# Cosine attention and MLP mixer on one core: two channel groups begun a slot earlier, token mixing in bunches, a cast moved, the last group halved

## The chip, the core and the metric

The kernel runs on one NeuronCore of a Trainium2 chip. The metric is the time on the device of one execution, in microseconds (us). Before the change the median of three runs is 408.05 us.

The engines have names in two styles. TensorE (PE in the profile) multiplies matrices. VectorE is DVE, ScalarE is ACT, GpSimd is POOL, and SyncE is SP, which issues most of the transfers. Each engine works through its own instructions in order; semaphores tie the engines together. TensorE writes only to PSUM, and all other tiles lie in SBUF.

## The reference, cut to what matters

```python
q_n = q / (norm(q) + 1e-6);  k_n = k / (norm(k) + 1e-6)      # 8 batches, 12 heads, 448 x 64
attn = softmax(q_n @ k_n.T / tau)                            # tau = 0.1
x = (attn @ v), heads side by side                           # 8 x 448 x 768
h = relu(x.T @ w_tok1) @ w_tok2                              # 448 -> 256 -> 448, along the sequence
u = x + h.T
out = u + relu(u @ w_ch1) @ w_ch2                            # 768 -> 1536 -> 768, along the channels
```

Inputs and output are float32. The kernel holds the operands of all matrix products as float16 and sums in float32.

## The kernel before

**Attention in slots.** Two heads make a pair; a batch has 6 pairs (`NPAIR`), and 8 batches have 48 (`N`). The main loop runs over slots, one pair a slot: in slot i the scores and exponentials of pair i are made, the product with v of pair i-1 (`pv`, in two parts), and the norms and transposes of the pairs to come. Nothing is scheduled by a planner: the order of the calls in the source is the order on each engine.

Slots 0 to 12 run `opening(i)`. On TensorE a slot there is: `score(i, 0)` (4 matmuls of 448 columns, L261, tile pS), `pv(i-1)` (32 matmuls of 65 columns, L282, tile pO), `score(i, 1)`, and `tpose_pe(i+1)` (8 transposes of the next pair, L240, tile pT). VectorE copies pT to the tile qkT (L248), which `score(i+1, 0)` reads. ScalarE makes the exponentials, `expo(i, 0)` to `expo(i, 3)` (L268, 112x896 each). POOL squares q and k (L180) and scales them (`normalize`, L213) with the reciprocal that VectorE makes (`norm_rec`, L200 and L202). VectorE also sums the squares (`norm_sum`, L190, tile ssq), casts v (`recast`, L127, a tensor_reduce over an axis of length 1), and scales pO into x (L288 and L289). From slot 13 on, `slot(i)` does the same with the transposes by DMA (`tpose_dma`, on SP's queue).

**Mixing.** `mixer(b)` makes the jobs of batch b:

- token mixing, first product: `tok1` (4 matmuls of 384 columns, L313, tile pR; ReLU on ScalarE to tile r, L316), four jobs;
- token mixing, second product: `tok2(i, dh)` (L326 or, for tile 3, L331; tile pU), then the sum with x on VectorE (L335, tile u, float32); after the second half of a tile the cast to float16, on VectorE for odd i (L339) and on ScalarE for even i (L341), and a transpose of the cast tile by DMA to the tile uT, on SP's queue;
- channel mixing, first product: `ch1(ct)` (a group of 6 matmuls, L379, tile pG; ReLU on ScalarE to gT, L381), twelve jobs;
- channel mixing, second product: `ch2(i, dh)` (a group of 12 matmuls of 384 columns, L388, tile pF; sum on VectorE, L392; then the store).

An even batch has three tiles of 128 rows, an odd one four; tile 3 holds the last 64 rows of both. So an odd batch has eight `tok2` jobs and an even one six.

For batch 0 the token mixing is not in the queue: it is done a pair at a time within slots 2 to 6 (`tok1_pair`, L351; `tok2_pair`, L362; `u_pair`, L370). `u_pair` writes the float16 sum of one pair and starts its transpose to `uT[:, pj]` on SP's queue. The sixth of the `uT` parts, `DT` = 6, is that of the last pair.

**The queue of jobs.** `spread(jobs, 6)` puts jobs into the list `todo` and sets `gap`, the sum of their costs over 30. `fill()`, called five times a slot, adds `gap` to a credit and pops jobs while the credit is above zero. After slot 6 the list is an empty job of 1.6 and the first eight `ch1` jobs of batch 0; the other four are kept as `late`. After slots 12, 18, 24, ... the list is what is late, the token jobs of the next batch merged with `ch2` jobs of the batch before (`held`), and the `ch1` jobs of the next batch. For an odd batch the merge gives four `tok1`, one `ch2`, four `tok2`, one `ch2`, four `tok2`, four `ch2`. What is left at the end runs after the last slot.

**PSUM.** The pool `ps` has four buffers, shared by pT, pO, pR, pU, pG and pF; `pss` has two for the scores. A tile waits until a buffer has been read out.

**Weights.** w_tok1 and w_tok2 are loaded in float32 and cast: `w1_cast` on VectorE, `w2_cast(0)` and `w2_cast(1)` on ScalarE (L139), in slots 1 and 2, each ahead of `score(i, 1)` and the exponentials that follow it. w_ch1 and w_ch2 come by DMAs from POOL's queue in slots 1 to 11.

Of the kernel before, what the change touches and what calls it, by code (L numbers as in the profile page):

```python
# [9 lines left out]
FP32 = mybir.dt.float32  # L10
FP16 = mybir.dt.float16
AF = mybir.ActivationFunctionType
ALU = mybir.AluOpType
# [10 lines left out]
def kernel(  # L24
# [19 lines left out]
    nc = tc.nc  # L44

    B, H, S, E = q.shape
    D = H * E
# [249 lines left out]
    def mixer(b):  # L297
        e, g = b % 2, b // 2
        xt = x16[g]
        t0, nt = (0, 3) if e == 0 else (3, 4)  # L300
        W = nt * 128
        r16[b] = mix.tile([128, TT, D], FP16, name="r16", tag="r16", bufs=2)
        u32 = mix.tile([128, nt, D], FP32, name="u32", tag="u32", bufs=2)
        u16 = mix.tile([128, nt, D], FP16, name="u16", tag="u16")
        uT = mix.tile([128, DT, W], FP16, name="uT", tag="uT")
        gT = mix.tile([128, CT, W], FP16, name="gT", tag="gT")

        def tok1(tt, dh):
            def job():
                pR = ps.tile([128, DH], FP32, name="pR", tag="ps")  # L310
                ks = [(4 * e + t, t) for t in range(3)] + [(3, 3 + e)]
                for n, (xi, wi) in enumerate(ks):
                    nc.tensor.matmul(pR[:], w1t[:, wi, tt * 128:(tt + 1) * 128],  # L313
                                     xt[:, xi, dh * DH:(dh + 1) * DH],
                                     start=(n == 0), stop=(n == 3))
                nc.scalar.activation(out=r16[b][:, tt, dh * DH:(dh + 1) * DH], in_=pR[:],  # L316
                                     func=AF.Relu)
            return 0.66, job

        def tok2(i, dh):  # L320
            def job():
                pU = ps.tile([128, DH], FP32, name="pU", tag="ps")
                for tt in range(TT):
                    if i != 3:
                        c0 = 128 * (i % 4)
                        nc.tensor.matmul(pU[:], w2t[:, tt, c0:c0 + 128],  # L326
                                         r16[b][:, tt, dh * DH:(dh + 1) * DH],
                                         start=(tt == 0), stop=(tt == TT - 1))
                    else:
                        for h in range(2):  # L330
                            nc.tensor.matmul(pU[64 * h:64 * h + 64], w2t[:, tt, S - 64:S],  # L331
                                             r16[2 * g + h][:, tt, dh * DH:(dh + 1) * DH],
                                             start=(tt == 0), stop=(tt == TT - 1))
                cols = slice(dh * DH, (dh + 1) * DH)
                nc.vector.tensor_tensor(out=u32[:, i - t0, cols], in0=pU[:], in1=xt[:, i, cols],  # L335
                                        op=ALU.add)
                if dh == NDH - 1:
                    if i % 2:
                        nc.vector.tensor_copy(out=u16[:, i - t0, :], in_=u32[:, i - t0, :])  # L339
                    else:  # L340
                        nc.scalar.copy(out=u16[:, i - t0, :], in_=u32[:, i - t0, :])  # L341
                    nc.sync.dma_start_transpose(
                        out=uT[:, :, (i - t0) * 128:(i - t0 + 1) * 128], in_=u16[:, i - t0, :])
            return 0.33, job

        def tok1_pair(pj):
            cols = slice(2 * pj * E, 2 * pj * E + 128)
            pR = ps.tile([128, TT, 128], FP32, name="pR", tag="ps")
            for tt in range(TT):
                for t in range(4):  # L350
                    nc.tensor.matmul(pR[:, tt, :], w1t[:, t, tt * 128:(tt + 1) * 128],  # L351
                                     xt[:, t, cols], start=(t == 0), stop=(t == 3))
            nc.scalar.activation(out=r16[b][:, :, cols], in_=pR[:], func=AF.Relu)

        pUs = {}

        def tok2_pair(pj):
            cols = slice(2 * pj * E, 2 * pj * E + 128)
            pU = ps.tile([128, nt, 128], FP32, name="pU", tag="ps")
            for i in range(nt):  # L360
                for tt in range(TT):
                    nc.tensor.matmul(pU[:, i, :], w2t[:, tt, i * 128:(i + 1) * 128],  # L362
                                     r16[b][:, tt, cols], start=(tt == 0), stop=(tt == TT - 1))
            pUs[pj] = pU

        def u_pair(pj, half):
            cols = slice(2 * pj * E, 2 * pj * E + 128)
            u = u16[:].rearrange("p t d -> p (t d)").rearrange("p (j x) -> p j x", j=NPAIR)[:, pj]
            o = u.rearrange("p (t e) -> p t e", t=nt) if half else u32[:, :, cols]
            nc.vector.tensor_tensor(out=o, in0=pUs[pj][:], in1=xt[:, 0:nt, cols], op=ALU.add)  # L370
            if half:
                nc.sync.dma_start_transpose(
                    out=uT[:, pj, :].rearrange("d (t m) -> d t m", t=nt), in_=u)

        def ch1(ct):
            def job():
                pG = ps.tile([128, W], FP32, name="pG", tag="ps")
                for dt in range(DT):
                    nc.tensor.matmul(pG[:], wc1t[:, dt, ct * 128:(ct + 1) * 128], uT[:, dt, :],  # L379
                                     start=(dt == 0), stop=(dt == DT - 1))  # L380
                nc.scalar.activation(out=gT[:, ct, :], in_=pG[:], func=AF.Relu)  # L381
            return 6 * W / 2400, job

        def ch2(i, dh):
            def job():
                pF = ps.tile([128, DH], FP32, name="pF", tag="ps")
                for ct in range(CT):
                    nc.tensor.matmul(pF[:], gT[:, ct, (i - t0) * 128:(i - t0 + 1) * 128],  # L388
                                     wc2t[:, ct, dh * DH:(dh + 1) * DH],
                                     start=(ct == 0), stop=(ct == CT - 1))  # L390
                o = u32[:, i - t0, dh * DH:(dh + 1) * DH]
                nc.vector.tensor_tensor(out=o, in0=pF[:], in1=o, op=ALU.add)  # L392
                end = b == B - 1 and i == t0 + nt - 1
                if dh == NDH - 1 or end:
                    store(i, slice(dh * DH, (dh + 1) * DH) if end else slice(0, D), end)
            return 1.96, job

        def store(i, cols, end):
            if i == 3:
                parts = [(h, 64 * h, S - 64, 64) for h in range(2)]  # L400
            else:
                f0 = 128 * (i % 4)
                parts = [(e, f - f0, f, n) for f, n in f_segments(f0, f0 + 128)]
            for z, (h, m, f, n) in enumerate(parts):
                rows = out[2 * g + h].rearrange("(p c) d -> c p d", c=NCH)
                queue = nc.scalar if end and z else nc.sync
                queue.dma_start(out=rows[f // P, f % P:f % P + n, cols],
                                in_=u32[m:m + n, i - t0, cols])

        if b == 0:  # L410
            front = (tok1_pair, tok2_pair, u_pair)
        else:
            front = [tok1(tt, dh) for dh in range(NDH) for tt in range(TT)]
            front += [tok2(i, dh) for i in range(t0, t0 + nt) for dh in range(NDH)]
        return (front, [ch1(ct) for ct in range(CT)],
                [ch2(i, dh) for i in range(t0, t0 + nt) for dh in range(NDH)])

# [58 lines left out]
    def opening(i):  # L476
# [10 lines left out]
        squares(i + 3)  # L487
        if i in wide:
            wide[i]()
        fill()  # L490
        if i >= 1:
            pv(i - 1, 0)
            pv(i - 1, 1)
        norm_rec(i + 2)
        if i in (1, 2):
            w2_cast(i - 1)
        r_, u_, add = first[0] if first else (None,) * 3
        done = [i - 2] if 2 <= i <= NPAIR else []
        if done:
            r_(i - 2)  # L500
# [1 line left out]
        score(i, 1)  # L502
        expo(i, 2)
        expo(i, 3)
        tpose_pe(i + 1)
        if i == NPAIR:
            r_(i - 1)
# [1 line left out]
        for pj in done:  # L509
            u_(pj)  # L510
        if i == NPAIR + 1:
            first[0][2](NPAIR - 1, False)
        for half in (True, False):
            for pj in done:
                if half or pj != NPAIR - 1:
# [46 lines left out]
    for i in range(N + 1):  # L562
# [13 lines left out]
                tpose_dma(i + 1)  # L576
            slot(i)
        if i == NPAIR:
            spread([(1.6, lambda: None)] + first[1][:8], NPAIR)
            late, held = first[1][8:], first[2]  # L580
        elif i and i % NPAIR == 0:
            front, c1, c2 = mixer(i // NPAIR - 1)
            spread(late + merge(front, held[:-3]) + held[-3:] + c1, NPAIR)
            late = []
            held = c2
    for _, job in todo + held:
# [36 lines left out]
```

## Time and profile before

| | |
|---|---|
| median of 3 runs | 408.05 us (406.93 to 409.0) |
| the profiled execution, in all | 408.18 us |
| its span, first to last instruction | 406.0 us |
| TensorE busy | 382.7 us, 94% of the span |
| ScalarE busy | 261.5 us, 64% |
| VectorE busy | 234.7 us, 58% |
| POOL busy | 196.2 us, 48% |
| granted TensorE clock, mean | 0.994 |

The times in all views are microseconds from the start of the span. A line of the timeline gives start, duration, engine, source line, operation, output and inputs, shapes and count; a bracket at its end gives the idle time of the engine before it and who ended it. Several equal instructions that follow each other are merged into one line. TensorE's matmuls overlap, so that a merged duration is a little longer than the time from its start to the next line's start. The chain of waits goes back from the last instruction to what released it, and gives time on the chain instead of durations.

### The profile page before, as it was taken

The page shows a single profiled execution, that of the slowest core. Times are in us where ns is not written, and L with a number is a line of the kernel's source. Part 1 is how long each engine was busy: PE and PEld are TensorE (multiplying, and loading weights), DVE is VectorE, ACT ScalarE, POOL GpSimd, SP SyncE. Part 2 cuts the span into 40 slices and gives each one's busy share as a digit, 9 for nine tenths or more (in the row PEclk, how much of TensorE's full clock was granted, in tenths as well). Part 3 has the DMA queues.
Part 4 walks back from the last instruction along what each step waited for, and adds up shares of the span by engine and source line. Part 5 has one row for each costly group of instructions (what it writes and reads, how often), then busy time and mean ns, then how long its engine had stood idle before and what let it go on. Part 6 is the DMA issues. An engine that isn't in the chain of part 4 may idle for free.

```text
span 406.0 us, 8998 instructions
## 1 busy us (share of the span) xinstructions
PE 382.7 (94%) x3592; PEld 219.4 (54%) x3592; DVE 234.7 (58%) x534; ACT 261.5 (64%) x451; POOL 196.2 (48%) x205
## 2 busy tenths in 40 slices
PE   2798799899999999999999999999999999999996
PEld 1465566555545555555555565555545556655453
DVE  5879978557544765467634766558644773161022
ACT  6799879865767557856687567756676665521400
POOL 3979979826544647443734655644653520000000
PEclk9999989999999999999999999999999999999999
DMA  7999999939963698529773597539972352026023
GB/s 240 260 234 213 227 293 227 242 99 190 228 135 92 160 216 203 139 79 199 225 185 101 144 189 233 131 80 191 245 157 68 78 123 84 2 61 134 0 48 109
DMA packets 97305, 63.57 MB, mean 157 GB/s; under 512 B 57520, under 2 KB 93808, under 8 KB 97264
## 3 DMA queue, kind: packets, MB, share of 16 engines
q1 hardware_dynamic: 93952, 58.14, 59.7%
q0 software_dynamic: 3184, 4.72, 6.7%
q8 instruction: 28, 0.46, 0.5%
q14 instruction: 13, 0.11, 0.1%
q10 hardware_dynamic: 128, 0.15, 0.1%
HBM read 43.38 MB, written 11.01 MB: 134 GB/s over the span
## 4 chain that ended last, share of the span: by engine, by line
PE 81%; DVE 12%; DMA 4%; ACT 2%; issue 1%; SPq 0%; DVEq 0%
PE pG L379 27%; PE pF L388 27%; PE pO L282 10%; PE pS L261 9%; PE pR L313 5%; PE pU L326 3%; DVE ssq L190 2%; DVE x L289 2%; DMA kl<-in_k_dram 1%; DVE qkT L248 1%; DVE u L370 1%; ACT pE L268 1%; DMA ql<-in_q_dram 1%; DMA w2s<-in_moe_w_tok_dram 1%; DVE u L335 1%; DVE rec L288 1%
## 5 line engine op out<-in xcount | busy, mean ns | idle before, releaser
L268 ACT ACTIVATE pE<-pS 112x896 f16<-112x896 f32 x192 | 164.8, 913 | 35.3 <-PE pS L261 34.7
L379 PE MATMUL pG<-uT,wc1t 128*128 128x384 f16 (+1 forms) x576 | 121.4, 355 | 0.0
L388 PE MATMUL pF<-wc2t,gT 128*128 128x384 f16 x672 | 116.6, 326 | 0.2
L213 POOL TENSOR_TENSOR qkn<-ql,rn 112x512 f16<-112x512 f32 x47 | 49.0, 1043 | 130.6 <-DVE rn L202 109.6
L388 PEld LDWEIGHTS <-gT 128*128 128x128 f16 x672 | 63.5, 98 | 47.0 <-issue 7.3
L381 ACT ACTIVATE gT<-pG 128x384 f16<-128x384 f32 (+1 forms) x96 | 52.4, 547 | 44.8 <-PE pG L379 43.9
L379 PEld LDWEIGHTS <-wc1t 128*128 128x128 f16 x576 | 51.6, 98 | 51.4 <-issue 11.0
L392 DVE TENSOR_TENSOR u<-pF,u 128x384 f32<-128x384 f32 x56 | 31.1, 555 | 78.0 <-PE pF L388 77.7
L261 PE MATMUL pS<-qkT 64*112 64x448 f16 x384 | 60.3, 385 | 9.8 <-DVE qkT L248 5.1
L282 PEld LDWEIGHTS <-pE 112*128 112x128 f16 x1536 | 59.0, 99 | 16.1 <-issue 5.6
L282 PE MATMUL pO<-v,pE 112*128 112x65 f16 x1536 | 62.8, 196 | 0.0
L288 DVE RECIPROCAL rec<-pO 128x6 f32<-128x6 f32 x96 | 17.5, 182 | 76.1 <-PE pO L282 75.2
L190 DVE TENSOR_REDUCE ssq<-sq 112x16 f32<-112x1024 f32 (+1 forms) x50 | 58.5, 1171 | 4.2 <-ACT sq L178 3.1
L180 POOL TENSOR_TENSOR sq<-ql 112x512 f32<-112x512 f32 x46 | 48.7, 1058 | 5.6 <-DMA ql<-in_q_dram 5.6
L213 POOL TENSOR_TENSOR qkn<-kl,rn 112x512 f16<-112x512 f32 x47 | 49.0, 1042 | 0.0
L180 POOL TENSOR_TENSOR sq<-kl 112x512 f32<-112x512 f32 x46 | 48.3, 1051 | 0.0
L289 DVE TENSOR_TENSOR x<-pO,rec 128x384 f16<-128x384 f32 x96 | 40.9, 426 | 3.3
L261 PEld LDWEIGHTS <-qkT 64*112 64x112 f16 x384 | 19.1, 128 | 35.6 <-issue 22.6
L127 DVE TENSOR_REDUCE v<-vl 112x512 f16<-112x512 f32 x40 | 25.5, 640 | 0.0
L335 DVE TENSOR_TENSOR u<-pU,x 128x384 f32<-128x384 f32 x50 | 25.4, 545 | 0.1
L341 ACT CAST u<-u 128x768 f16<-128x768 f32 x14 | 11.6, 832 | 20.9 <-DVE u L335 20.9
L194 ACT ACTIVATE ln<-ssq 112x16 f32<-112x16 f32 (+1 forms) x49 | 10.9, 222 | 17.5 <-DVE ssq L190 17.2
(43 smaller groups left out, 183.4 us busy)
## 6 DMA issues: line engine op xcount, KB each, us to landing
ql<-in_q_dram SPq DMA_DIRECT2D x48, 224.0 KB, 3.6
kl<-in_k_dram SPq DMA_DIRECT2D x48, 224.0 KB, 4.0
vl<-in_v_dram SPq DMA_DIRECT2D x48, 224.0 KB, 4.2
out_dram<-u SPq DMA_DIRECT2D x8, 336.0 KB, 3.4
wc1t<-in_moe_w_ch_dram POOLq DMA_DIRECT2D x4, 576.0 KB, 7.9
wc2t<-in_moe_w_ch_dram POOLq DMA_DIRECT2D x3, 768.0 KB, 10.1
out_dram<-u SPq DMA_DIRECT2D x8, 288.0 KB, 3.8
out_dram<-u SPq DMA_DIRECT2D x7, 240.0 KB, 3.0
```

The source lines that it names most:

```text
L180: nc.gpsimd.tensor_mul(out=s["sq"][:, j], in0=a, in1=a)
L190: nc.vector.tensor_reduce(out=small(i, "ssq")[:, j], in_=st_[i]["sq"][:, j], axis=AXX.X, op=ALU.add)
L213: eng.tensor_tensor(out=t[:, j].rearrange("p c g e -> p g c e"), in0=s[nm][:], in1=_bcast_free(rn, E), op=ALU.mult)
L261: nc.tensor.matmul(pS[:, h, 0:S], s["T"][64 * h:64 * h + 64, 1, c * P:(c + 1) * P], s["T"][64 * h:64 * h + 64, 0, :], start=True, stop=True)
L268: nc.scalar.activation(out=s["p"][:, c], in_=s["pS"][c][:, :, 0:S], func=AF.Exp, scale=inv_tau)
L282: nc.tensor.matmul(pO[:, n, h, :], s["p"][:, c, h, c0:c0 + 128], s["v16"][:, NCH * h + c, 0:E + 1], start=(c == 0), stop=(c == NCH - 1))
L289: nc.vector.tensor_tensor(out=xt[hp:hp + nr, t0:t0 + len(ts), d0:d0 + 2 * E].rearrange("p t (h e) -> p t h e", h=2), in0=pO[m0:128, :, :, ...
L335: nc.vector.tensor_tensor(out=u32[:, i - t0, cols], in0=pU[:], in1=xt[:, i, cols], op=ALU.add)
L379: nc.tensor.matmul(pG[:], wc1t[:, dt, ct * 128:(ct + 1) * 128], uT[:, dt, :], start=(dt == 0), stop=(dt == DT - 1))
L381: nc.scalar.activation(out=gT[:, ct, :], in_=pG[:], func=AF.Relu)
L388: nc.tensor.matmul(pF[:], gT[:, ct, (i - t0) * 128:(i - t0 + 1) * 128], wc2t[:, ct, dh * DH:(dh + 1) * DH], start=(ct == 0), stop=(ct == C ...
L392: nc.vector.tensor_tensor(out=o, in0=pF[:], in1=o, op=ALU.add)
```

## The change

There are five edits.

1. The first two `ch1` groups of batch 0 leave the queue. In slot 7 (`NPAIR + 1`), after the transposes of pair 8, their matmuls over parts 0 to 3 of uT are issued; in slot 8, ahead of the first `fill`, those over parts 4 and 5 and the two ReLUs. The queue after slot 6 holds `ch1` jobs 2 to 9 instead of 0 to 7, and two jobs are late instead of four.
2. `w2_cast(0)` stands behind `expo(1, 2)` and `expo(1, 3)` in slot 1. `w2_cast(1)` stays.
3. For odd batches the token jobs stand in another order among the `ch2` jobs: four `tok1` and two `tok2`, one `ch2`, three `tok2`, one `ch2`, three `tok2`, four `ch2`.
4. The cast of u to float16: tiles 1 and 5 on VectorE as a tensor_reduce instead of a copy; tile 3 on ScalarE instead of VectorE; the other tiles stay on ScalarE.
5. The very last `ch2` group is computed as two groups of 12 matmuls of 192 columns, each with its own sum and its own stores.

```diff
-                    if i % 2:
-                        nc.vector.tensor_copy(out=u16[:, i - t0, :], in_=u32[:, i - t0, :])
+                    if i in (1, 5):
+                        recast(u16[:, i - t0, :], u32[:, i - t0, :])
                     else:
                         nc.scalar.copy(out=u16[:, i - t0, :], in_=u32[:, i - t0, :])
...
+        def ch1_part(ct, d0, d1):
+            if not d0:
+                pGs[ct] = ps.tile([128, W], FP32, name="pG", tag="ps")
+            for dt in range(d0, d1):
+                nc.tensor.matmul(pGs[ct][:], wc1t[:, dt, ct * 128:(ct + 1) * 128], uT[:, dt, :],
+                                 start=(dt == 0), stop=(dt == DT - 1))
+            if d1 == DT:
+                nc.scalar.activation(out=gT[:, ct, :], in_=pGs[ct][:], func=AF.Relu)
+
         def ch1(ct):
...
+            return 6 * W / 2400, partial(ch1_part, ct, 0, DT)
...
                 end = b == B - 1 and i == t0 + nt - 1
-                if dh == NDH - 1 or end:
-                    store(i, slice(dh * DH, (dh + 1) * DH) if end else slice(0, D), end)
+                parts = 2 if end and dh == NDH - 1 else 1
+                for z in range(parts):
+                    cols = slice(dh * DH + z * DH // parts, dh * DH + (z + 1) * DH // parts)
+                    pF = ps.tile([128, DH // parts], FP32, name="pF", tag="ps")
+                    for ct in range(CT):
+                        nc.tensor.matmul(pF[:], gT[:, ct, (i - t0) * 128:(i - t0 + 1) * 128],
+                                         wc2t[:, ct, cols],
+                                         start=(ct == 0), stop=(ct == CT - 1))
+                    o = u32[:, i - t0, cols]
+                    nc.vector.tensor_tensor(out=o, in0=pF[:], in1=o, op=ALU.add)
+                    if end:
+                        store(i, cols, end)
+                if dh == NDH - 1 and not end:
+                    store(i, slice(0, D), end)
...
+        if i == NPAIR + 2:
+            for ct in range(2):
+                first[0][3](ct, DT - 2, DT)
         fill()
...
-        if i in (1, 2):
-            w2_cast(i - 1)
+        if i == 2:
+            w2_cast(1)
...
         expo(i, 2)
         expo(i, 3)
+        if i == 1:
+            w2_cast(0)
         tpose_pe(i + 1)
...
         if i == NPAIR + 1:
-            first[0][2](NPAIR - 1, False)
+            add(NPAIR - 1, False)
+            for ct in range(2):
+                g_(ct, 0, DT - 2)
...
         if i == NPAIR:
-            spread([(1.6, lambda: None)] + first[1][:8], NPAIR)
-            late, held = first[1][8:], first[2]
+            spread([(1.6, lambda: None)] + first[1][2:10], NPAIR)
+            late, held = first[1][10:], first[2]
         elif i and i % NPAIR == 0:
             front, c1, c2 = mixer(i // NPAIR - 1)
-            spread(late + merge(front, held[:-3]) + held[-3:] + c1, NPAIR)
+            if (i // NPAIR) % 2:
+                mid = merge(front, held[:-3]) + held[-3:]
+            else:
+                mid = front[:6] + held[:1] + front[6:9] + held[1:2] + front[9:] + held[2:]
+            spread(late + mid + c1, NPAIR)
```

In the changed kernel's traces `ch1`'s matmuls are at L381 and its ReLU at L384, `ch2`'s matmuls at L397 and its sum at L401.

More of the change, by code (lines that the diff above doesn't have):

```diff
@@ L373, in u_pair @@
                     out=uT[:, pj, :].rearrange("d (t m) -> d t m", t=nt), in_=u)
-        def ch1(ct):
[L376 to L382, printed above, removed]
+        pGs = {}
@@ L384, in ch2 @@
         def ch2(i, dh):
             def job():
[L386 to L392, printed above, removed]
@@ L410, in mixer @@
         if b == 0:
-            front = (tok1_pair, tok2_pair, u_pair)
+            front = (tok1_pair, tok2_pair, u_pair, ch1_part)
         else:
@@ L494, in opening @@
         norm_rec(i + 2)
-        if i in (1, 2):
-            w2_cast(i - 1)
-        r_, u_, add = first[0] if first else (None,) * 3
+        if i == 2:
+            w2_cast(1)
+        r_, u_, add, g_ = first[0] if first else (None,) * 4
         done = [i - 2] if 2 <= i <= NPAIR else []
```

## The prediction

> **What bounds the kernel now.** I read the page first, parts 2 and 4.
>
> ```profile
> span 406.0 us, 8998 instructions
> ...
> PE   2798799899999999999999999999999999999996
> ...
> PEclk9999989999999999999999999999999999999999
> ...
> PE 81%; DVE 12%; DMA 4%; ACT 2%; issue 1%; SPq 0%; DVEq 0%
> ```
>
> One character is 10.15 us. From the eighth (71 us) TensorE is full to the end; before that it has gaps, and in the sixth slice its clock fell. So work taken out of the full part counts in full, and work put into an early gap is free if nobody waits behind it. The fall is at slots 7 and 8; the timeline and the windows show it.
>
> ```profile
> 47.29 0.57 PE L240 MATMUL pT<-id,qkn 112*128 112x112 f16 x8
> 48.77 0.62 DVE L248 COPY qkT<-pT 128x896 f16<-128x896 f16 x1
> 49.45 0.63 PE L261 MATMUL pS<-qkT 64*112 64x448 f16 x4 [1.59 <-DVE qkT L248]
> 50.02 2.10 PE L379 MATMUL pG<-uT,wc1t 128*128 128x384 f16 x6
> 53.48 0.20 DVE L288 RECIPROCAL rec<-pO 128x6 f32<-128x6 f32 x1 [1.90 <-PE pO L282]
> 54.57 1.14 PE L379 MATMUL pG<-uT,wc1t 128*128 128x384 f16 x6
> ...
> 46.57:49.98 3.41, 1.59 (x16) 1.00 1.26 274
> 49.98:53.40 3.42, 3.42 (x35) 0.50 1.13 220
> ...
> 32.92:36.33 3.41, 2.69 (x39) 1.00 1.39 191
> ```
>
> Slot 7 ends with 1.59 us in which TensorE waits for VectorE's copy of the transposed pair. The window lines read: stretch, its length, TensorE busy (instructions), granted clock, DMA. The stretch with 1.59 us of work is followed by one of 3.42 us at half clock; a stretch with 2.69 us was not. So six pG matmuls took 2.04 us on the chain there, against 0.98 later, and VectorE waited for pO until 53.48.
>
> The timeline and the chain around 180 us show the second place:
>
> ```profile
> 179.53 1.37 DVE L339 CAST u<-u 128x768 f16<-128x768 f32 x1
> 185.08 0.56 DVE L339 CAST u<-u 128x768 f16<-128x768 f32 x1
> 184.18 0.50 PE L326 MATMUL pU<-r,w2t 128*128 128x384 f16 x2 [0.65 <-DVE x L289]
> ```
>
> In batch 3 VectorE falls behind four token products in a row and a slow cast, and TensorE waits for a PSUM buffer. Batch 5 repeats it at 272 to 277. By matmul starts, TensorE loses 0.22, 0.25 and 0.82 us over its usual pace, 1.28 per batch.
>
> **The change part by part.** Durations are of the profiled execution: 406.0 in the span, 408.18 in all, so 2.1 outside; the median is 408.05, so I subtract gains from that.
>
> *The w2 cast, slot 1.* Now:
>
> ```profile
> 17.51 0.99 ACT L139 CAST w2t<-w2s 128x448 f16<-128x448 f32 x1 [1.01 <-DMA w2s<-in_moe_w_tok_dram]
> 18.40 3.35 ACT L268 ACTIVATE pE<-pS 112x896 f16<-112x896 f32 x4
> ```
>
> Two exponentials stand behind a wait of 1.01 for a load and the 0.99 cast. Put ahead, they start at 17.1, when their scores are done, and end at 18.8; the cast follows to 19.8. The next score waits for them and for the copy of 18.45 to 19.07: it starts at 19.1 instead of 19.37, its second half 0.65 earlier. pv, VectorE and POOL behind it follow. ScalarE itself gains only 0.3, but its next exponentials had gaps before them. Gain 0.65 (0.2 to 0.7) up to slot 7, where slots 3 to 6 keep a VectorE rhythm of 4.44.
>
> *Two groups begun in slot 7.* Eight pG matmuls go between the transposes and score(8,0). At 0.162 each (the rate inside a group) that is 1.30. They wait for two PSUM buffers, freed by VectorE at 47.70 and 48.23, and for the transposed pair 3, issued at 39.90 and landed 7.2 later, at 47.1. So they run from 47.7 to 49.1 and are over before VectorE's copy ends at 49.39. score(8,0), queued behind them, is not late. All that makes them free is this gap; without it they cost 1.30.
>
> *The same groups ended in slot 8.* Four matmuls (0.65) now precede the group that the queue pops there. They need pair 5, whose transpose was issued at 46.22 and landed 4.3 later, at 50.5. The stretch before 49.98 now holds 1.59 + 1.30 = 2.89 us of work, more than the 2.69 that stayed warm, so I take full clock. If the landing stays at 50.5: the last three run to 50.98, a group 0.98, three quarters of pv 0.74: pO at 52.70 against 53.45, a gain of 0.75 that contains the cast's 0.65. If the landing moves up by 0.65 with its issue, 1.40. I take 1.1 for both edits together. ScalarE gets three ReLUs (0.49 each) ahead of expo(8,2); they end at 53.4, expo(8,2) started at 54.09. The second pv half and the next transposes wait for the first two ReLUs, done by 52.9, before they are needed. Slots 9 to 12 pass the 1.1 on: POOL, 4.8 a slot and full, starts 55.45 on VectorE's reciprocal, which comes earlier; its loads landed over 2 us ahead.
>
> *Moved out of the full part.* Twelve matmuls of 0.162 leave the stretch after 75 us: 1.95, sure unless TensorE stops being full there.
>
> [...]
>
> *Bunches and casts.* Six jobs, one output group, three, one, three in place of four, one, four, one, four. Tile 3's cast moves to ScalarE (0.83, four times, idle there a third of the time), so VectorE loses 1.37 just where TensorE waited, and an output group (1.95) comes before the third bunch. Tiles 1 and 5 become a reduce: the same shape took 0.94 as w1's cast beside a busy POOL, against 0.56 to 1.37. For tile 5, 0.56 becomes 0.94, at most 0.4 off-path. SP's transpose of tile 3 now waits for ScalarE, and loads and transposes stand behind it; the cast is done within 2 us of its sum, and scores come later. Of 2 x 1.28 = 2.57 I take 1.8 (0 to 2.57). Batches 1 and 7 have no stall to lose. In batch 1 three of the four ReLUs stand behind two exponentials: the last ends about 2.85 after score begins to end, TensorE gets there at 2.65: cost 0.2 (0 to 2.2).
>
> [...]
>
> *Last group halved.* The last add is 0.56 for 384 columns and 0.29 for 128 on half the partitions: about 0.3 for 192. Twelve more matmuls of half the width keep the sum of columns. The two stores more, one on SP's and one on ScalarE's queue, are the first half's and go out under the second half's 0.98. Gain 0.26 plus a smaller store: 0.3 (0 to 0.5).
>
> Sum: 1.1 + 1.95 + 1.8 - 0.2 + 0.3 = 4.95. 408.05 - 4.95 = **403.1**.
>
> **The rivals.**
>
> *The clock falls all the same* (its stretches of 3.41 need not lie the same way in another execution; pairs landing late leave a new gap). Then nine pG matmuls at 0.32 run from 50.5 to 53.4, and pO, at full clock again, ends at 54.1: -0.7 in place of +1.1, 404.9. For it: the fall at so small a gap. Against: 2.89 busy.
>
> *The token stall moves instead of going.* VectorE still has seven sums, a cast and ssq (1.2) in a row; the wait turns up at another buffer. 1.8 becomes 0: 404.9. Both together: -0.7 + 1.95 - 0.2 + 0.3 = 1.35, 406.7.
>
> *Slower: token products wait for ScalarE.* Today an output group of 1.95 stands between the last token ReLU and the first product that reads it. Now nothing does. If that ReLU stands behind two exponentials in batches 1, 3 and 5, TensorE waits 1.72 + 0.49 = 2.21 three times, 6.63, and the token gain is gone: 1.1 + 1.95 + 0.3 - 6.63 = -3.3, 411.3. It decides from 1.1 us a batch. Against it: in the built order of batches 3 and 5 all four ReLUs stand ahead of the exponentials, and a score (0.52) lies between; only in batch 1 do three stand behind.
>
> **How the numbers follow.** Forecast 0.61, clock 0.12, token stall 0.12, both 0.07, ScalarE 0.08. The forecast's own range is 401.6 (all upper ends: 1.4 + 1.95 + 2.57 + 0.5) to 404.6; the two rivals at 404.9 belong in the range, which I close at 401.4 and 406.4. Half a per cent, about what a measurement of this kernel can tell from no change, is 2.0: faster means under 406.0. The first three cases are: 0.85. Same is the double case, 0.07; slower 0.08.
>
> **What would show it.** Right: eight pG matmuls between the transposes and the score of slot 8, the clock at 1.00 there, pO of slot 8 about a microsecond earlier, TensorE waits in batches 3 and 5 under 0.5 each, TensorE's last matmul near 397. Wrong: a new half-clock stretch, a pG waiting on the transposed pairs for over 1 us, pU waiting for r, or an end that moves by less than the groups' 1.95.

## The result

| | before | after |
|---|---|---|
| median, six executions each on the same chip | 407.49 us (406.56 to 409.95) | 402.21 us (401.06 to 402.95) |
| the profiled execution, in all | 408.18 us | 402.3 us |
| its span | 406.0 us | 400.5 us |

The medians differ by 5.3 us, where 4.95 was forecast. The ratio on record is 0.9848, with a 95% interval of 0.9819 to 0.9878, in which the ratio of the two medians, 0.9870, lies as well: faster. The median of 402.2 stands against a forecast of 403.1; of these 0.9 us, 0.56 are the kernel before, whose median is now 407.49 where the prediction started from 408.05. Lines of the page of the changed kernel:

```profile
span 400.5 us, 9027 instructions
...
PE   2788999899999999999999999999999999999996
...
PEclk9989999999999999999999999999999999999999
...
PE 84%; DVE 9%; ACT 4%; DMA 1%; issue 1%
```

VectorE's share of the chain has gone from 12% to 9%, the DMAs' from 4% to 1%. In the sixth slice, where the clock row had an 8, it has a 9. But the third slice (20 to 30 us) now has the 8, which the prediction had not foreseen. The timeline of TensorE around slots 7 and 8 (start, duration, engine, line, tiles; idle time before in brackets):

```profile
47.06 0.57 PE L240 MATMUL pT<-id,qkn 112*128 112x112 f16 x8
47.57 1.46 PE L381 MATMUL pG<-uT,wc1t 128*128 128x384 f16 x8
49.22 0.63 PE L261 MATMUL pS<-qkT 64*112 64x448 f16 x4 [0.19 <-DVE qkT L248]
49.78 1.80 PE L381 MATMUL pG<-uT,wc1t 128*128 128x384 f16 x10
51.42 1.15 PE L282 MATMUL pO<-v,pE 112*128 112x65 f16 x32
```

The eight matmuls stand in the gap, where the wait of 1.59 is now 0.19, and the ten that follow wait for nothing. The windows give the clock (stretch, length, TensorE busy, then the other engines, granted clock, DMA):

```profile
21.62:25.03 3.41, 1.79 (x18) 1.15 (x18) 2.82 (x8) 3.38 (x7) 3.28 (x4) 1.00 1.13 258
25.03:28.45 3.42, 3.15 (x42) 2.70 (x41) 2.30 (x6) 2.67 (x6) 3.04 (x4) 0.50 1.28 279
45.51:48.92 3.41, 3.19 (x43) 1.96 (x38) 3.21 (x9) 3.25 (x7) 3.23 (x5) 1.00 1.02 182
48.92:52.34 3.42, 3.23 (x46) 2.21 (x45) 2.42 (x4) 3.13 (x7) 3.42 (x4) 1.00 0.98 191
```

Slots 7 and 8 stay at full clock. The half clock is at 25 us instead, behind a stretch in which TensorE worked for 1.79 us, mostly because a token product of batch 0 waited 1.13 us for ScalarE:

```profile
21.99 0.57 PE L240 MATMUL pT<-id,qkn 112*128 112x112 f16 x8
23.69 0.49 PE L362 MATMUL pU<-r,w2t 128*128 128x128 f16 x6 [1.13 <-ACT r L353]
...
89.61 2.11 PE L397 MATMUL pF<-wc2t,gT 128*128 128x384 f16 x12 [0.22 <-DVE u L335]
```

```profile
22.37 0.99 ACT L139 CAST w2t<-w2s 128x448 f16<-128x448 f32 x1
23.26 0.37 ACT L353 ACTIVATE r<-pR 128x256 f16<-128x256 f32 x1
```

On ScalarE the ReLU that is waited for (tile r) stands behind the second w2 cast, which the change left in its place. The line at 89.61 is a small wait that stays in batch 1. The ledger of the two profiles takes the start of the first score of each slot and sums what the changed kernel is ahead:

| step | predicted | measured | where it is read |
|---|---|---|---|
| cast and groups together, slots 0 to 13 | 1.1 | 1.13 | 0.23 up to slot 8, 0.90 between slots 8 and 9 |
| work moved out, less the wait in batch 1 | 1.75 | 1.58 | between slots 13 and 18 |
| token mixing, batches 3 and 5 | 1.8 | 2.38 | 1.19 at slot 27, 1.19 at slot 39 |
| last group | 0.3 | 0.43 | end of the span |
| outside the span | 0 | 0.36 | 2.14 to 1.78, by spans of 406.04 and 400.52 |
| sum | 4.95 | 5.88 | 408.18 to 402.3 |

### The profile page after: what moved, and what is told of

It reads as the page before. It is cut to its first block, busy times and chain, and to the rows that moved or that the text cites. A ratio compares the mean times of both kernels' runs of the same rounds, so it can differ in the third digit from the quotient of the medians.

```text
span 400.5 us, 9027 instructions
## 1 busy us (share of the span) xinstructions
PE 379.6 (95%) x3604; PEld 218.0 (54%) x3604; DVE 233.0 (58%) x531; ACT 263.8 (66%) x455; POOL 194.6 (49%) x205
## 4 chain that ended last, share of the span: by engine, by line
PE 84%; DVE 9%; ACT 4%; DMA 1%; issue 1%
PE pF L397 28%; PE pG L381 27%; PE pO L282 10%; PE pS L261 10%; PE pR L313 5%; PE pU L326 3%; DVE ssq L190 3%; ACT pE L268 2%; DVE x L289 2%; DVE qkT L248 1%; DVE u L370 1%; PE pU L331 1%; DMA ql<-in_q_dram 1%; DVE rec L288 1%; DVE rn L202 0%
## 5 line engine op out<-in xcount | busy, mean ns | idle before, releaser
L381 PE MATMUL pG<-uT,wc1t 128*128 128x384 f16 (+1 forms) x576 | 120.3, 353 | 0.0
L397 PE MATMUL pF<-wc2t,gT 128*128 128x384 f16 (+1 forms) x684 | 116.7, 324 | 0.5 <-DVE u L335 0.2
L397 PEld LDWEIGHTS <-gT 128*128 128x128 f16 x684 | 64.0, 98 | 46.7 <-issue 6.5
L384 ACT ACTIVATE gT<-pG 128x384 f16<-128x384 f32 (+1 forms) x96 | 52.3, 547 | 43.6 <-PE pG L381 42.6
L381 PEld LDWEIGHTS <-wc1t 128*128 128x128 f16 x576 | 51.4, 98 | 50.5 <-issue 9.3
L401 DVE TENSOR_TENSOR u<-pF,u 128x384 f32<-128x384 f32 (+1 forms) x57 | 31.3, 549 | 69.2 <-PE pF L397 69.1
L282 PEld LDWEIGHTS <-pE 112*128 112x128 f16 x1536 | 57.8, 99 | 16.8 <-issue 6.6
L180 POOL TENSOR_TENSOR sq<-ql 112x512 f32<-112x512 f32 x46 | 47.8, 1038 | 5.9 <-DMA ql<-in_q_dram 5.9
L341 ACT CAST u<-u 128x768 f16<-128x768 f32 x18 | 15.0, 832 | 19.7 <-DVE u L335 19.7
L313 PE MATMUL pR<-x,w1t 128*128 128x384 f16 x112 | 20.4, 327 | 0.0
```

What stands on the lines that cost most here:

```text
L180: nc.gpsimd.tensor_mul(out=s["sq"][:, j], in0=a, in1=a)
L282: nc.tensor.matmul(pO[:, n, h, :], s["p"][:, c, h, c0:c0 + 128], s["v16"][:, NCH * h + c, 0:E + 1], start=(c == 0), stop=(c == NCH - 1))
L381: nc.tensor.matmul(pGs[ct][:], wc1t[:, dt, ct * 128:(ct + 1) * 128], uT[:, dt, :], start=(dt == 0), stop=(dt == DT - 1))
L384: nc.scalar.activation(out=gT[:, ct, :], in_=pGs[ct][:], func=AF.Relu)
```

## The experiments

Every kernel below has plain copies in place of the transposing DMAs; "base" is the kernel before in that form. The edits are shown shortened, and some in words. A figure "ahead" is the ledger of its one profiled execution against that of the base. The ratios are to the kernel before on the same chip. The base, the whole change, the groups and both token edits together ran on one chip; the order, the casts of u, the first run of the cast alone and the smaller bunch on a second; the others on a third.

**The base, and the whole change on it.**

```diff
-  nc.sync.dma_start_transpose(out=uT[:, pj, :]..., in_=u)
+  nc.sync.dma_start(out=uT[:, pj, :], in_=u)
```

> The kernel before with every transposing DMA replaced by plain copies of the same size on the same queue (the transposition is left out, so the layout of what is multiplied is not the reference's); it is the base of the experiments. TensorE, VectorE, ScalarE and POOL have the same instructions. Every theory: the same stalls (1.59 us in slot 7, 1.28 in batches 3 and 5), and a time within 2 us of the kernel before, since no landing of a transpose is on the chain.

> The changed kernel with the same plain copies. If landings of the transposes play no part, it is as much faster than the base as the changed kernel than the kernel before: 5.0 to 5.8 us, of it 0.35 by slot 4, 0.9 at slot 9, 1.6 by slot 18, 1.2 each in batches 3 and 5, 0.4 behind TensorE's end. If the landing of pair 5 held slot 8 (a term of the prediction), up to 0.4 more.

Measured: base 407.91, ratio 0.9987 (0.9965 to 1.0009); whole change 401.42, ratio 0.9855 (0.9827 to 0.9883). The base behaves as the kernel before, with the same fall of the clock (0.50 from 50.69 to 54.10), and the change is worth as much on it. So parts can be tried on it.

**The groups alone.**

```diff
+  # slot 7: add(NPAIR - 1, False); for ct in range(2): g_(ct, 0, DT - 2)
+  # slot 8: for ct in range(2): first[0][3](ct, DT - 2, DT)
-  spread([(1.6, lambda: None)] + first[1][:8], NPAIR)
+  spread([(1.6, lambda: None)] + first[1][2:10], NPAIR)
```

> The base with only the first edit: two channel groups begun in slot 7 and ended in slot 8. Theory A (the gains of the five edits are local and add up): the score of slot 9 begins about 0.9 to 1.1 us earlier than in the base (full clock and a filled gap), slot 18 another 1.95, and the time falls by 2.9 us (2.4 to 3.4). Theory B (the gain in slot 8 is only that one execution had no half-clock stretch there, and others have it all the same): the groups' own 1.95 us stay and the time falls by 1.95 us or less.

Measured: 405.93, ratio 0.9956 (0.9938 to 0.9974). The moved work is there: 1.87 ahead is won between slots 13 and 18. But slot 8 loses 0.28 though its clock is full (1.00 from 49.75 to 53.17). The timeline of TensorE:

```profile
49.54 0.64 PE L262 MATMUL pS<-qkT 64*112 64x448 f16 x4 [0.19 <-DVE qkT L249]
51.21 1.91 PE L382 MATMUL pG<-uT,wc1t 128*128 128x384 f16 x10 [1.03 <-DMA uT<-u]
```

The chain names the transfer:

```profile
45.03 6.14 DMA uT<-u
```

The groups wait 1.03 us for pair 4, issued at 45.03 and landed at 51.17; the matmul behind the first then waits about 0.1 for pair 5, issued at 45.61 and landed at 51.45, 5.84 later. In the changed kernel the two took 4.12 and 3.38, and nothing waited. Over all profiles pair 5 took 3.38 to 5.84. This is the term "if the landing moves" of the prediction, and it came out differently from profile to profile. By the medians the groups alone are 1.98 faster than the base. That is theory B's size, but not by its reason: slot 8 had full clock and lost the gain to the landing.

**The token edits, together and one by one.**

```diff
+  mid = front[:6] + held[:1] + front[6:9] + held[1:2] + front[9:] + held[2:]   # order
-  if i % 2: nc.vector.tensor_copy(out=u16..., in_=u32...)                       # casts
+  if i in (1, 5): recast(u16..., u32...)
```

> The base with only the token jobs' order and the casts of u changed. Theory A: TensorE's stalls in batches 3 and 5 (1.28 us each) shrink to about 0.1 to 0.3 each, batch 1 loses 0.4, the time falls by 2.0 us (1.6 to 2.6). Theory D (the stalls go only because everything from slot 13 on comes earlier in the full change): they stay, and the time falls by less than 0.8 us.

> Edit: only the order of the token products, in bunches with output groups between, without the other engines for the casts, on the plain-copy base. Both together gave 1.20 in each of batches 3 and 5, 2.39 in all. Theory A, the order does it: with an output group of 1.95 ahead of the third bunch VectorE catches up in spite of its cast of 1.37; the gain is 2.0 to 2.4 and slots 26 to 27 move by 1.0 to 1.2. Theory B, the cast does it: the cast of 1.37 still stands in VectorE's way, the order alone saves the two small waits, 0.22 and 0.25 a batch, 0.9 in all, and the wait of 0.82 stays.

> Edit: only the casts of u: tile 3 on ScalarE, tiles 1 and 5 as a reduce on VectorE; the order of the token products stays as before, on the plain-copy base. Theory A (order): the four products in a row still fill the four PSUM buffers faster than VectorE adds, the gain is under 0.5 in all. Theory B (cast): VectorE has 1.37 less to do just ahead of the wait of 0.82, the gain is 0.8 in each of batches 3 and 5, 1.6 in all, at slots 26 to 27 and 38 to 39.

Measured: both 404.36, ratio 0.9920 (0.9890 to 0.9951); order alone 405.77, 0.9909 (0.9876 to 0.9941); casts alone 405.64, 0.9918 (0.9887 to 0.9949). The medians do not tell these apart, since the start of an execution scatters by more (see the clock below); the ledger does. Both together win 1.19 and 1.20 in batches 3 and 5, the order alone 1.19 and 1.20, the casts alone 0.50 and 0.51. In batch 1, where theory A had a loss of 0.4, both together lose 0.05. So the order does it and the casts add nothing to it: theory A for the order, between the two for the casts, which gave 0.5 a batch where A said under 0.25 and B 0.8. VectorE of the kernel with the order alone, tile 3 of batch 3:

```profile
174.43 1.02 DVE L336 TENSOR_TENSOR u<-pU,x 128x384 f32<-128x384 f32 x2 [1.48 <-PE pU L332]
175.49 0.56 DVE L340 CAST u<-u 128x768 f16<-128x768 f32 x1
```

Tile 3's cast takes 0.56, not 1.37, in the place to which the new order has moved it. In the kernel before it runs at 179.53, beside POOL's operations at 179.45 and 180.45, of 1.04 and 1.35; that these lengthen it was not tried. How much of the 1.19 is this shorter cast and how much the smaller bunches, these runs do not part. And TensorE there:

```profile
180.40 0.89 PE L283 MATMUL pO<-v,pE 112*128 112x65 f16 x24
181.22 0.59 PE L262 MATMUL pS<-qkT 64*112 64x448 f16 x4
181.74 1.15 PE L327 MATMUL pU<-r,w2t 128*128 128x384 f16 x6
183.03 2.12 PE L389 MATMUL pF<-wc2t,gT 128*128 128x384 f16 x12
```

From the start of the six pU to that of pF it is 1.29, and six matmuls of 0.162 are 0.97: 0.32 is still lost. With the casts alone, eight pU matmuls still stand in one row.

**The cast alone, twice.**

```diff
-  if i in (1, 2): w2_cast(i - 1)          # ahead of score(i, 1)
+  if i == 2: w2_cast(1)
   expo(i, 3)
+  if i == 1: w2_cast(0)
```

> Edit: only the first w2 cast is moved behind the exponentials of slot 1, on the plain-copy base. Theory of the prediction: the start gains 0.65 (0.2 to 0.7) and keeps it to the end, so 407.3 beside 407.9 for the plain-copy base. What the changed kernel's ledger suggests: 0.35 by slot 4, so 407.55. Rival, the landing: slot 8 starts its channel groups when pair 5 has landed, which follows SP's queue and the loads on it and not the cast; then the lead seen at slots 4 to 8 is gone at slot 9 and the time is that of the base. In the profile: the start of the first score of slot 4 and of slot 9 against those of the base (31.41 and 56.89); a half-clock stretch that falls elsewhere has to be set aside.

> Edit: as in the run of the cast alone, once more. There the five executions agreed within 0.25 us, all without a stretch of half clock, though slot 7 still has a gap that should be followed by one for about 6 of 10 positions of the stretches. Theory A, chance: the position of the stretches is free, and this time some executions have the stretch and take 1.57 longer; their spread is that of the base, and the median is 405.3 to 407. Theory B, the moved cast fixes where the stretches lie: again all within 0.3 us at 0.985 to 0.99 of the time of before.

Measured: first 405.25 (405.17 to 405.42), ratio 0.9896 (0.9876 to 0.9917); the second time, on another chip, 407.15 (405.19 to 408.45), ratio 0.9964 (0.9941 to 0.9987). The edit does not fix the clock, then, though a difference between the chips is not excluded: the second time the executions fall in two groups, five with a mean clock of 0.998 or more at 405.19 to 406.27, and seven with 0.992 or less at 407.13 to 408.45. The profile of the second run belongs to the second group. Its windows:

```profile
20.86:24.27 3.41, 1.98 (x24) 1.24 (x22) 2.61 (x8) 3.38 (x8) 3.41 (x5) 1.00 1.12 287
24.27:27.68 3.41, 2.92 (x37) 2.17 (x36) 2.29 (x4) 3.38 (x7) 3.41 (x4) 0.50 1.12 265
27.68:31.10 3.42, 3.42 (x31) 2.42 (x28) 2.00 (x7) 2.30 (x4) 1.84 (x3) 0.50 1.13 280
```

At slot 3 it was 2.22 ahead, and 0.11 at slot 4. What the edit itself removes shows on ScalarE in slot 1; first the base, then the cast alone (the first of its two runs):

```profile
18.34 0.99 ACT L139 CAST w2t<-w2s 128x448 f16<-128x448 f32 x1 [1.86 <-DMA w2s<-in_moe_w_tok_dram]
19.23 1.72 ACT L269 ACTIVATE pE<-pS 112x896 f16<-112x896 f32 x2
```

```profile
17.45 1.72 ACT L269 ACTIVATE pE<-pS 112x896 f16<-112x896 f32 x2 [0.72 <-PE pS L262]
19.07 1.00 ACT L139 CAST w2t<-w2s 128x448 f16<-128x448 f32 x1
```

Without the edit ScalarE waited for w2s between 0.18 and 1.86 us in the seven profiles, as that load landed; with it, in none of the others. The prediction took 1.01, the one wait it saw.

**The clock alone.** Nothing of the change, only unread work in the gap of slot 7:

```diff
   first[0][2](NPAIR - 1, False)
+  for _ in range(2):                       # two PSUM tiles pD
+      for j in range(4): nc.tensor.matmul(pD, wc1t[:, 0, 128*j:128*j+128], wc1t[:, 1, 0:384], ...)
```

> Edit: nothing of the change; eight matmuls whose result nobody reads (128 x 384, as the channel groups) go into the gap of slot 7, on the plain-copy base. Theory, the clock: in ten profiles each stretch of 3.41 us with TensorE busy for 1.81 or less was followed by a stretch at half clock, and none with 2.24 or more was; slot 7 has such a stretch for about 62% of the positions that the stretches can have, and 1.3 us of work fills it. So slot 8 never falls to half clock, the gain is 1.57 where it fell, and the median goes from 407.9 to about 407.0 with no half clock near 50 us in the profile. Rival, the gap is not free (the matmuls hold two PSUM buffers that the next token sums need): 0.3 to 1.3 slower. Rival, the clock falls for another reason: still half clock in the profile at 49 to 53.

Measured: 406.57 (405.31 to 408.67), ratio 0.9969 (0.9947 to 0.9992), 1.3 us below the kernel before. The base itself has 0.9987 (0.9965 to 1.0009), so the times alone do not part the two. Windows of the base, and then of this kernel:

```profile
47.28:50.69 3.41, 1.59 (x16) 0.90 (x16) 3.21 (x10) 3.03 (x6) 3.22 (x4) 1.00 1.02 246
50.69:54.10 3.41, 3.41 (x31) 2.14 (x30) 1.73 (x3) 2.54 (x5) 3.08 (x4) 0.50 1.03 207
```

```profile
46.80:50.21 3.41, 3.04 (x25) 1.57 (x23) 3.21 (x10) 3.00 (x7) 3.23 (x5) 1.00 1.03 247
50.21:53.62 3.41, 3.41 (x54) 2.46 (x54) 2.92 (x7) 3.21 (x7) 2.89 (x3) 1.00 1.12 254
```

The ledger wins 1.58 between slots 8 and 9 (0.67 to 2.25) and nothing behind; the 0.67 ahead at slot 4 comes before the edit and is scatter of the start. One profile of each could be chance, so all fourteen profiles are taken together: of the seven with this gap open, four have half clock at slots 7 and 8, where six pG matmuls take 1.80 to 2.04 (the other three: 1.08 to 1.31); of the seven with matmuls in it, none. So eight matmuls that compute nothing shorten slot 8, with the clock at 1.00 where the base has 0.50. In the whole change the same place gave 0.90: 1.58 less the four matmuls, 0.65, that end the groups there.

**Work against the half clock behind slot 2, on the whole change.**

```diff
   tpose_pe(i + 1)
+  if i == 2: six matmuls of 128 x 256, w1t by w1t, unread
```

> Edit: the whole change, and six matmuls of 128 x 256 whose result nobody reads in slot 2, ahead of the token product that waits 1.13 us for ScalarE's ReLU. Theory, the clock: with the whole change slot 2 is the only place left with a stretch of 3.41 us that is busy for 1.81 or less (for about 4 of 10 positions of the stretches), and executions with such a stretch took 403.7 to 403.9 against 401.0 to 401.6. The 0.65 us of work lifts it above 2.2: no half clock after the first full one, every execution at 401.0 to 401.6. Rival, the work is in the way: where the clock is still low in slot 2 the six take 1.3, and the time is 0 to 0.6 longer than 401.4.

Measured: 401.86 (401.61 to 402.15), ratio 0.9849 (0.9819 to 0.9878). All six executions have a mean clock of 0.998 or more and lie within 0.54; of the six of the whole change, four had that (401.03 to 401.58) and two not (403.65 and 403.88). The stretch of slot 2 is lifted as meant:

```profile
22.74:26.15 3.41, 3.16 (x39) 2.12 (x37) 2.64 (x9) 3.41 (x6) 2.77 (x4) 1.00 1.14 239
26.15:29.56 3.41, 2.96 (x58) 2.23 (x55) 3.21 (x9) 3.30 (x8) 3.04 (x4) 1.00 0.91 265
```

No execution is high here. With two high of six before, six without one could still be chance. The good ones are about half a microsecond longer, as the rival had it, though on another chip. By the median it is no faster than the whole change, and none of the versions tried is.

**A smaller last bunch, on the whole change.**

```diff
-  front[9:] + held[2:]
+  front[9:11] + held[2:3] + front[11:] + held[3:]
```

> Edit: the whole change, and the last bunch of the token products cut in two with an output group between, so that the order is six, group, three, group, two, group, one. In the whole change TensorE still waits 0.31 to 0.38 for VectorE's sums ahead of the output group behind the last bunch, in batches 1, 3 and 5. Theory, the wait is one for a free PSUM buffer and a bunch of two leaves one free: it goes in all three batches, 1.0 in all, 400.4 beside 401.4. Rival, VectorE is late as such (a cast of 0.95 in that place) and the wait comes back behind the last product: no change.

Measured: 404.19 (403.51 to 404.85), ratio 0.9870 (0.9847 to 0.9893). The wait of batch 1 is gone (0.38 more between slots 13 and 18 than the whole change), but batches 3 and 5 give +0.72 and -0.44 where the whole change gives +1.19 each. TensorE behind the output groups of batch 5, and SP's queue:

```profile
278.68 3.90 PE L398 MATMUL pF<-wc2t,gT 128*128 128x384 f16 x23
282.42 0.41 PE L283 MATMUL pO<-v,pE 112*128 112x65 f16 x8
282.76 0.59 PE L262 MATMUL pS<-qkT 64*112 64x448 f16 x4
285.25 1.46 PE L382 MATMUL pG<-uT,wc1t 128*128 128x512 f16 x6 [1.90 <-DVE ssq L190]
```

```profile
280.12 0.40 SPq L165 DMA_DIRECT2D vl<-in_v_dram  x1
280.62 0.66 SPq L343 DMA_DIRECT2D uT<-u  x1
```

The same place of the whole change:

```profile
277.09 0.65 SPq L343 DMA_DIRECT2D uT<-u  x1
277.79 0.64 SPq L165 DMA_DIRECT2D ql<-in_q_dram  x1
```

The releaser named, ssq, has nothing to do with pG. What pG reads is the last uT, issued at 280.62 and landed at 285.16, 0.09 before it starts. Two things came together. An output group of 1.95 was taken from behind the last product and put ahead of it, and that group had helped to hide the transfer: in the whole change (on the base) the last uT of batches 3 and 5 lands 2.36 and 1.98 us before it is read. And the later transfer stands behind the three loads of the next pair on SP's queue, where it stood ahead of them; it took 4.54 instead of 2.75 (in batch 3, 3.93 instead of 2.82). With 2.75 it would have landed at 283.37, and the wait would have been about 0.1. That the loads are what lengthened it was not tried alone. Neither the theory nor the rival had this.

**Attention output first in slot 8, on the whole change.**

```diff
+  pv(i - 1, 0); pv(i - 1, 1)      # slot 8: ahead of
   first[0][3](ct, DT - 2, DT)     # the rest of both groups
   fill()
-  pv(i - 1, 0); pv(i - 1, 1)
```

> Edit: the whole change, but in slot 8 the attention output of the pair before goes ahead of the rest of the two channel groups and of the group that the queue pops. Theory: VectorE, which waits 1.00 us for pO there, and POOL behind it (1.62 us) go on earlier by the time of ten matmuls, 1.6, less VectorE's cast that stands before: 0.5 to 1.0 earlier from slot 9 on, and the wait for the landing of pair 5 is covered by 1.1 us of other work; 400.5 to 401.0. Rival, ScalarE: its three ReLUs now end 1.1 later, the exponentials of the second half of slot 8 stand behind them, and the next scores come later: no change, or up to 0.5 slower.

Measured: 402.56 (401.56 to 403.71), ratio 0.9870 (0.9833 to 0.9906): no gain. Between slots 8 and 9 it wins 0.65, the whole change 0.93. TensorE:

```profile
49.76 1.15 PE L283 MATMUL pO<-v,pE 112*128 112x65 f16 x32
50.74 0.81 PE L382 MATMUL pG<-uT,wc1t 128*128 128x384 f16 x4
52.08 1.15 PE L382 MATMUL pG<-uT,wc1t 128*128 128x384 f16 x6 [0.52 <-DVE x L290]
```

pO is 1.6 us earlier, as meant, but now both pO tiles and the two open pG tiles hold all four PSUM buffers; the queue's group waits until VectorE has read pO out, and VectorE has ssq and its cast of v ahead of that. The rival had the sign, by another engine. That PSUM is the cause rests on this one wait.

## Why the prediction was right or wrong, point by point

**Right in what bounds the kernel, and in sign.** The forecast case came: eight matmuls in the gap, full clock in slot 8, VectorE taking up pO of slot 8 at 52.35 where it was 53.48, no token wait over 0.5 in batches 3 and 5, TensorE's last matmul ending at 397.07 ("near 397"). The time is 0.9 below the forecast and inside its range. But one sign that the prediction named for being wrong came too, a new half-clock stretch, in a place that none of its terms covers. (Of its page, the busy row has an 8 in the eighth slice: TensorE is full from about 81 us, not 71. No term hangs on that.)

**The step that failed is the token term: 1.8 forecast, 2.38 measured.** It is the largest error. The prediction had most of it in view, 1.28 a batch, and took 1.8 of the 2.57, for waits that might move. The runs showed that 1.19 goes in each batch. The 1.28 was itself short: the last two pU, from 184.18 to 184.64, take 0.46 where two matmuls of 0.162 are 0.32, and that loss was not counted; so 1.19 can go while 0.32 stays. The reason was also half wrong: it named the cast of 1.37 taken off VectorE "just where TensorE waited", while the order alone yields as much as both edits, and shortens the cast besides; the casts alone yield 0.50. The reduce for tile 5, counted as a possible loss, cost nothing that the ledger shows: both edits together give what the order gives.

**The front, 1.1 against 1.13, was right as a sum but not in its parts.** Predicted were 0.65 from the cast, with the rest from slot 8. Measured are 0.23 up to slot 8 and 0.90 in it. The cast's step read one landing of w2s as if it were fixed. Worse, the 1.54 that the changed kernel was ahead at slot 3 came mostly from an earlier full clock (18.21 instead of 26.09 us), and the half clock at 25 us took 1.31 of it back. The cast is not needed for either: the order alone and both token edits, which leave the cast in place, had full clock by 19.93 (two pS matmuls in 0.40, against 0.62 at 20.18 in the kernel before) and at 17.92, and a half-clock stretch behind it. In slot 8 luck helped: pair 5 was issued 0.10 earlier and landed 0.99 earlier, in 3.38 us, the shortest of all profiles, so that nothing waited. That the parts add up to 1.1 is luck.

**The clock step was right in direction, by too little evidence.** From one stretch with 1.59 and one with 2.69, the prediction took it that 2.89 would stay warm. Now it is shown by the work that computes nothing: with 3.04 in that stretch the next was at 1.00. What the step missed is chance: sliding stretches of 3.41 us along TensorE's work in the profile before, about 62% of their positions have one with 1.85 or less in slots 7 and 8, and 33% one with 1.81 or less; one with 1.82 kept full clock (below), so the share is known no better than that. By this estimate there is no half clock to lose in the other positions, so that the term is 1.58 in some executions and 0 in others; four of the seven profiles with the gap open had it. In the same way about 38% of the positions in the changed kernel's profile have a stretch with 1.85 or less in slots 1 to 3. The two high executions of the whole change, with mean clocks of 0.995 and 0.992, may be of that kind; no profile of them shows where.

**The work moved, 1.95, and the wait in batch 1, 0.2.** The groups alone gave 1.87; the whole change gives 1.58, which is 0.37 short of 1.95. It is not the ReLU that was named: it is the output group, which reads nothing of VectorE's sum u and so waits for that sum to free a PSUM buffer (the line at 89.61), and a smaller last bunch wins 0.38 back. Both token edits without the groups lose only 0.05 there; why it takes the groups as well was not followed.

**The tail, 0.3, gave 0.43.** The last adds in the changed kernel:

```profile
396.12 0.36 DVE L401 TENSOR_TENSOR u<-pF,u 128x192 f32<-128x192 f32 x1 [0.36 <-PE pF L397]
397.11 0.36 DVE L401 TENSOR_TENSOR u<-pF,u 128x192 f32<-128x192 f32 x1 [0.63 <-PE pF L397]
```

An add of 192 columns is 0.36 instead of the 0.3 estimated, but what follows TensorE's end falls from 4.04 to 3.45; the halved group itself costs TensorE 0.16. That split was not tried alone. The 0.36 outside the span was not in the sum, and no run explains it.

**The rivals.** The clock did fall all the same, but in slot 3, not in slot 8. The token wait did not move. The token products of batches 1, 3 and 5 do not wait for ScalarE's ReLU; the one that does, 1.13 in slot 2, belongs to batch 0, and no rival had it. Open is how much of the 0.23 up to slot 8 is the cast's: its two runs, 0.9896 and 0.9964, differ by more than the edit is worth.

## What to carry to other kernels

Read the granted clock in stretches laid end to end from its first change, and ask how busy each was, not only how long a gap is: a gap of 1.59 us ahead of a dense part gave 1.87 for work moved into it (the groups alone, which lost 0.28 in slot 8) and, in another run, 1.58 for the clock (work that computes nothing). Price a step that hangs on a transfer's landing with the scatter of landings over several executions; one profile gives one draw, and five executions that agree within 0.25 us can be followed by twelve that spread over 3.3. When moving work across a queue, look for the transfer that it hid: one group of 1.95 us put on the other side of the last product, with the transfer then queued behind three loads, turned a gain of 1.19 into a loss of 0.44.

## What the runs showed of the hardware

**Half clock came behind partly busy stretches.** The stretches of 3.41 us are laid end to end from the clock's first change. At full clock, half clock followed stretches in which TensorE was busy for 1.15 us (both token edits), 1.59 (the kernel before, and the base), 1.79 (the changed kernel) and 1.98 (the cast alone, second run). In that second run one with 1.82 kept full clock: 24 pO matmuls took 0.74 behind it, against 1.33 at half clock in the kernel before. In the first ten profiles together each stretch with 1.81 or less was followed by half clock, and none with 2.24 or more was. On the way up more work stood ahead of the change. Ahead of the first full clock (from about 9 us on) and at half clock, the stretches with full clock behind them had 3.15, 3.16 and, eight times, 3.34 to 3.42; one with 3.11 and seventeen with 3.00 or less had none behind them. These are counted in the kernel before, the changed kernel, the base, the whole change on it, the groups alone, both token edits and the cast's second run. The last stretches, at the kernel's end, are left out. The ends of matmuls are modelled, so the second decimal should not be trusted.

**The stretches lay differently from profile to profile.** Full clock was first granted between 17.45 us (the cast alone, second run) and 26.80 us (the base) after the start of the span, a scatter of 9 us. With the groups alone, the stretches with 2.84 and 2.76 had no full clock behind them; the next, with 3.41, had it, at 25.86. The profile has no clock record ahead of the first full clock, and its rows and means show 1.00 there; but four pS matmuls take 0.99 at 8.73 us in the kernel before, and 0.63 at 49.45. So a mean clock of 1.000 does not tell when the full clock began.

**Landings scatter.** The same transfer of pair 5, about 45 us into the kernel, took 3.38 to 5.84 us from issue to landing; whether the DMA transposes (3.38 and 4.27) or copies (3.59 to 5.84) made no difference that shows.
